# Attention followed by two MLPs on one core: scores of the 384- and 512-key tiles by head from fp32r parts, and products of zeros at the front

## The chip, the cores and the metric

One core of one Trainium2 chip. The metric is the device time of one execution in microseconds (us), as the median of three runs. TensorE is the matrix engine (PE in the rows, its weight loads PEld); DVE is VectorE, ACT is ScalarE, POOL is GpSimd, SP is the engine that issues most of the DMAs.

## The reference, cut to what matters

Three parts follow one another. Batch 4, 8 heads, 576 positions, 64 values per head; 2304 tokens of 512 values; hidden size 2048.

```python
scores = q @ k.T / sqrt(64)                    # per batch and head
scores = where(pos_i // 64 >= pos_j // 64, scores, -1e9)
attn   = softmax(scores);  x = attn @ v        # x: 2304 x 512 over the heads
h = x @ w_in;  g = s * relu(h)**2 + b;   x = g @ w_out      # first MLP
h = x @ w2_in; g = max(0.01*h, h);       out = g @ w2_out   # second MLP
```

The mask works on blocks of 64 positions: a query sees all keys of its own block and of the blocks before it.

## The kernel before, in words

**Tiles.** The 576 positions are cut into five tiles of 128 query positions, k = 0 to 4 (the last has 64). One tile over the four batches is a block of T = 512 tokens (256 for k = 4) of the MLPs. ORDER (line 165) runs ten blocks: the first MLP over the tiles 0, 1, 2, 4, 3, then the second over 0, 1, 2, 3, 4. Attention of a tile runs beside the first MLP of the block before it: attention of k = 1 beside block k = 0, k = 2 beside k = 1, k = 4 beside k = 2, and k = 3 (512 keys) beside block k = 4, the short one with T = 256. Only the attention of k = 0 has no MLP beside it; it is the front of the kernel (lines 467 to 545).

**MLP.** For each of 16 slices f of the hidden size, `m_in` (line 706) makes h with 12 products in fp32r (parts of x and of the weights, high and low: `xh`, `xl`; three products for each of four chunks), ScalarE and VectorE make from it the parts `gh` and `gl`, and `m_out` (line 751) makes 12 products into four banks y0 to y3 (line 765). The weights come as 64-bit words and are turned into parts by VectorE and ScalarE (`chunk`, lines 256 to 293). Results of the four y banks go through SBUF tiles `yo` of the pool "st" (line 777) to DRAM.

**Attention of a later tile** (`later_block`, line 552) is 16 units, one for each batch and pair of heads. The scores of a unit are fp32 products (`scores`, line 426; the profile shows two passes for each product). Two heads lie in one 128-row contraction: the tile `qz` holds for 64 query positions (half s of the tile) the columns of head 0 in its upper 64 rows and of head 1 in its lower 64 rows, with zeros elsewhere, so the 128 output rows are two heads times 64 positions. There is one product for each half, and it takes only the keys that this half sees: 320 and 384 for k = 2, 448 and 512 for k = 3. Each half has a PSUM bank of the pool "s" (two banks). Then come the maximum (line 391), its negative (394), exp with a running sum (400), 1/sum (406, 409), the product with it (422), transposes through bank "t" (445), their copy into `pt` (358, 360) and, for two units at once, the product with v (line 650), where the two heads write different halves of the output's partitions.

**Order.** A planner (class `Graph`, line 44) simulates the engines with costs written beside each step and takes, whenever an engine is idle, the ready step with the lowest due time; buffers are counted as in the pools. The sequence it finds is written out, and on the chip each engine runs its steps strictly in it. The cost estimates of attention (`att_pe`) and of the MLP blocks set the due times (`begin`).

**Front.** TensorE starts with 8 products of zeros (WARM, line 461) into the bank "h", which is also the bank of `m_in`; then come the four pairs of heads p of tile 0, whose scores stand in y0/y1, y2/y3, the two "s" banks, and y0/y1 again (line 511), with transposes through "t" and "h" and the product with v into "t".

Of the kernel before, what the change touches and what calls it, by code (L numbers as in the profile page):

```python
# [168 lines left out]
def kernel(  # L169
# [23 lines left out]
    scale = 1.0 / float(D) ** 0.5  # L193
    WARM, LATE, PACE, AHEAD = 8, 10, (6.0, 4.9), 3
    EARLY = NF - 1

    def sb(name, bufs):
        return ctx.enter_context(tc.tile_pool(name=name, bufs=bufs))

    def ps(name, bufs):  # L200
# [5 lines left out]
        "w": (sb("w", NF), NF), "st": (sb("st", 3), 3),  # L206
        "xf": (sb("xf", 4), 4), "xh": (sb("xh", 4), 4), "xl": (sb("xl", 4), 4),
        "g": (sb("g", 1), 1), "gh": (sb("gh", 2), 2), "gl": (sb("gl", 2), 2),
        "k": (sb("k", 2), 2), "v": (sb("v", 3), 3), "p": (sb("p", 2), 2), "pt": (sb("pt", 3), 3),
# [4 lines left out]
    G = Graph({k: n for k, (_, n) in pools.items()}, ("k", "v", "p", "pt", "s", "t", "h", "xf", "xh", "xl", "st"))  # L214
# [14 lines left out]
    qz = [const.tile([128, 2, 2, 64], F32, name=f"qz{i}") for i in range(3)]  # L229
# [4 lines left out]
    att_pe = [16 * (share[k] * 1.67e-3 + NQ[k] / 64 * (k + 1) * 0.21 + 0.15) for k in range(NB)]  # L234
# [118 lines left out]
    def memz(e, ap):  # L353
        e.memset(ap, 0.0)
# [9 lines left out]
    def both(n):  # L364
        return {"ACT": act(n), "DVE": dve(n)}

    qz_ok = [
        G.add({"POOL": 0.4}, lambda e, z=z: memz(e, z), due=14.0 if i else -99) for i, z in enumerate(qz)
    ]
    qz_free = [[q] for q in qz_ok]  # L370
# [90 lines left out]
    for i in range(WARM):  # L461
        G.add(
            {"PE": 0.43}, lambda e: e.matmul(out=wb()[:, :128], lhsT=qz[0][:, 0].rearrange("d h c -> d (h c)"),
                                             rhs=qz[0][:, 0].rearrange("d h c -> d (h c)"), start=True, stop=True),
            [qz_ok[0]], [wb] * (i == 0), [wb], -90,
        )
# [42 lines left out]
    for p in range(NP):  # L509
        due = 10.0 + 4.0 * p  # L510
        y0, y1 = [bank(key, "s") for key in (("y0", "y1"), ("y2", "y3"), ("s", "s"), ("y0", "y1"))[p]]
# [12 lines left out]
        tr = transposed(P, pcols, cells, pt, nrm, due, ("t", "h"))  # L524
        o = bank("t", "o")
# [24 lines left out]
    nq = [0]  # L550

    def later_block(blk):
# [5 lines left out]
        for u in range(NP * B):  # L558
            p, b = divmod(u, B)
            due = w0 + (u + 1) * (w1 - w0) / (NP * B)  # L560
            z = nq[0] % len(qz)
            nq[0] += 1
            K = buf("k", [128, S], F32)
            V = buf("v", [128, 5, 128], F32)
            ql = [
                G.add({"SP": 0.65}, lambda e, h=h, z=z, b=b, p=p: e.dma_start(
                    out=qz[z][64 * h:64 * h + 64, :ns, h], in_=qT[b, p, 64 * h:64 * h + 64, h, 128 * k:128 * k + NQ[k]].rearrange("d (s c) -> d s c", c=64)),
                    qz_free[z], due=due - 13, nbytes=32768)
# [20 lines left out]
            if k == 1:  # L589
                bk = bank("s", "s")  # L590
                cols = [(bk, 0, keys[0]), (bk, keys[0], keys[1])]
            elif k < NB - 1:
                cols = [(bank("s", "s"), 0, n) for n in keys]
            else:
                cols = None
            P = buf("p", [128, 1024], F32)
            q_ap = lambda j, z=z: qz[z][:, j].rearrange("d h c -> d (h c)")
            k_ap = lambda j, n, K=K: K()[:, :n]
            wide = nj * 128
            if cols:  # L600
                pads = G.add({"POOL": 0.2}, lambda e, P=P: memz(e, P()[:, keys[0]:keys[0] + 64]), [], [P], [], due - 6)
                sc = scores(k, [], [K], cols, q_ap, k_ap, [*ql, *kl], due, set())
                nrm = softmax(k, None, cols, P, [s * wide for s in range(ns)], due, sc)
                cells = [(s * wide + 128 * j, s) for j in range(nj) for s in range(ns)]
            else:
# [5 lines left out]
                for j in range(2):  # L611
                    def fn(e, j=j, bk=bk, K=K, z=z):
                        e.matmul(out=bk[j]()[:, :half], lhsT=qz[z][:, 0].rearrange("d h c -> d (h c)"), rhs=K()[:, half * j:half * j + half], start=True, stop=True)  # L613
                    sc.append(G.add({"PE": half * 1.67e-3 + 0.02}, fn, [*ql, *kl], [bk[j]], [K], due - 5))
# [20 lines left out]
            qz_free[z] = sc  # L635
# [9 lines left out]
            def av(e, pair=pair, o=o, n=n):  # L645
                for x, (b, V, pt, _) in enumerate(pair):
                    for j in range(nj):
                        for h in range(2):
                            r = pt()[:, j * ns * 128:(j + 1) * ns * 128].rearrange("k (s c) -> k s c", s=ns)[:, :, 64 * h:64 * h + 64]
# [208 lines left out]
```

## Time and profile before

| | us |
|---|---|
| median of three runs (lowest, highest) | 1018.62 (1015.87, 1020.55) |
| the profiled execution | 1019.93 |
| its span, from the first to the last instruction | 1018.1 |
| TensorE busy | 995.8 |
| VectorE, ScalarE, GpSimd busy | 452.9, 403.9, 93.3 |

The profile is of one execution. Its page gives the busy time of each engine and the same over 40 equal slices of the span, in tenths, with the clock granted to TensorE. The chain of waits follows the work that ended last back to its beginning, each piece with its start and its length; pieces of one line next to each other are merged. The timeline gives instructions in order of time. The length of a single matrix product in the timeline includes its way through the array, which overlaps the next one's; what a product costs in a dense row is the distance between starts, or the chain's piece divided by its count.

### The profile page before, as it was taken

The numbers are of one execution on the slowest core, as the hardware profiler recorded it, in microseconds if no ns is written. First come the engines' busy times: TensorE is split into PE (matmuls) and PEld (weight loads), VectorE is DVE, ScalarE is ACT, GpSimd is POOL, SyncE is SP. The second block draws the span as 40 slices with busy tenths as digits, with TensorE's granted clock in tenths as the row PEclk, the third lists the DMA queues.
The fourth block names the chain that finished last, engine by engine and source line by source line (L and its number), as shares of the span: only waits on it lengthen the run. The fifth ranks groups of instructions, "written<-read, shape, count | busy, mean of one in ns | idle before, by whom it ended". The sixth has DMA issues, their size and how long they took to land.

```text
span 1018.1 us, 14594 instructions
## 1 busy us (share of the span) xinstructions
PE 995.8 (98%) x5536; PEld 816.7 (80%) x5536; DVE 452.9 (44%) x855; ACT 403.9 (40%) x866; POOL 93.3 (9%) x238
## 2 busy tenths in 40 slices
PE   8799999999999999999999999999999999999997
PEld 7578787777777887777888888888888888888897
DVE  4889855443364434555455888413112211311211
ACT  3667754333353333443344766323122122222221
POOL 1021311111111111122310000000000000000000
PEclk7799999999999999999999999999999999999999
DMA  8872232222232333333324547002000200200010
GB/s 241 267 273 78 69 91 89 64 60 60 64 108 76 85 86 86 102 94 94 92 64 138 202 169 245 1 0 83 1 1 21 63 1 1 62 1 1 1 43 21
DMA packets 88645, 83.86 MB, mean 82 GB/s; under 512 B 28544, under 2 KB 71680, under 8 KB 88576
## 3 DMA queue, kind: packets, MB, share of 16 engines
q1 hardware_dynamic: 86128, 82.15, 26.1%
q10 hardware_dynamic: 2448, 0.79, 0.3%
q8 instruction: 44, 0.72, 0.3%
q14 instruction: 25, 0.20, 0.1%
HBM read 73.47 MB, written 9.44 MB: 81 GB/s over the span
## 4 chain that ended last, share of the span: by engine, by line
PE 92%; DVE 3%; ACT 2%; DMA 1%; issue 1%; POOL 0%; ACTq 0%; SPq 0%; DVEq 0%; POOLq 0%
PE h L716 38%; PE y L765 37%; PE s L430 6%; PE o L650 4%; PE t L445 4%; PE s L613 2%; PE o L530 1%; ACT p L400 1%; DVE nm L391 0%; DVE g L732 0%; POOL p L422 0%; DMA fk<-in_k_dram 0%; ACT g L734 0%; ACT w L279 0%; DMA fq<-in_q_dram 0%
## 5 line engine op out<-in xcount | busy, mean ns | idle before, releaser
L716 PE MATMUL h<-xh,w 128*128 128x512 f32 (+1 forms) x1280 | 455.6, 385 | 4.1 <-DVE g L732 2.0
L765 PE MATMUL y<-gh,w 128*128 128x512 f32 (+2 forms) x1280 | 369.4, 372 | 0.1
L716 PEld LDWEIGHTS h<-xh,w 128*128 128x128 f32 x1280 | 237.9, 189 | 55.2 <-DVE g L732 7.0
L765 PEld LDWEIGHTS y<-gh,w 128*128 128x128 f32 x1280 | 230.1, 188 | 41.8 <-issue 1.6
L765 PE MATMUL y<-gl,w 128*128 128x512 f32 (+2 forms) x640 | 236.2, 369 | 0.2 <-DVE gl L745 0.2
L716 PE MATMUL h<-xl,w 128*128 128x512 f32 (+1 forms) x640 | 235.9, 369 | 0.0
L745 DVE TENSOR_TENSOR gl<-g,gh 128x512 fp32r<-128x512 f32 (+1 forms) x80 | 51.0, 638 | 271.5 <-ACT g L744 271.5
L743 ACT ACTIVATE gh<-h 128x512 fp32r<-128x512 f32 (+1 forms) x80 | 44.3, 554 | 268.1 <-PE h L716 267.8
L716 PEld LDWEIGHTS h<-xl,w 128*128 128x128 f32 x640 | 121.0, 189 | 21.3 <-issue 2.6
L765 PEld LDWEIGHTS y<-gl,w 128*128 128x128 f32 x640 | 120.6, 188 | 21.1 <-DVE gl L745 0.4
L734 ACT ACTIVATE g<-h 128x512 f32<-128x512 f32 (+1 forms) x80 | 44.4, 555 | 135.7 <-PE h L716 134.7
L400 ACT ACTIVATE p<-s,nm 128x64 f32<-128x64 f32 (+7 forms) x128 | 62.8, 508 | 43.3 <-DVE nm L394 31.0
L422 POOL TENSOR_SCALAR p<-p,l 128x192 f32<-128x192 f32 (+3 forms) x95 | 59.0, 634 | 189.5 <-DVE l L409 136.0
L445 PE MATMUL t<-id_sb,p 128*128 128x128 f32 x400 | 67.1, 283 | 8.7 <-DVE p L415 5.5
L445 PEld LDWEIGHTS t<-id_sb,p 128*128 128x128 f32 x400 | 50.1, 145 | 29.5 <-issue 10.6
L430 PE MATMUL s<-k,qz 128*128 128x192 f32 (+2 forms) x192 | 70.8, 470 | 1.6 <-ACT p L400 1.5
L391 DVE TENSOR_REDUCE nm<-s 128x1 f32<-128x192 f32 (+3 forms) x104 | 53.4, 523 | 38.3 <-PE s L430 36.5
L732 DVE TENSOR_TENSOR g<-g,h 128x512 f32<-128x512 f32 (+1 forms) x52 | 32.8, 630 | 64.2 <-ACT g L734 63.8
L358 ACT ACTIVATE pt<-t 128x512 f32<-128x512 f32 (+2 forms) x67 | 33.7, 502 | 64.6 <-PE t L445 63.9
L360 DVE COPY pt<-t 128x512 f32<-128x512 f32 (+2 forms) x53 | 34.0, 641 | 52.0 <-PE t L445 51.6
L737 DVE TENSOR_TENSOR gl<-g,gh 128x512 fp32r<-128x512 f32 (+1 forms) x80 | 51.0, 637 | 11.7 <-ACT gh L736 10.2
L736 ACT ACTIVATE gh<-g 128x512 fp32r<-128x512 f32 (+1 forms) x80 | 47.1, 588 | 16.1 <-DVE g L732 14.6
(68 smaller groups left out, 709.8 us busy)
## 6 DMA issues: line engine op xcount, KB each, us to landing
early<-in_moe_w_in_dram SPq DMA_DIRECT2D x30, 512.0 KB, 3.8
early<-in_moe_w_out_dram SPq DMA_DIRECT2D x30, 512.0 KB, 4.8
v<-in_v_dram SPq DMA_DIRECT2D x32, 256.0 KB, 3.1
k<-in_k_dram SPq DMA_DIRECT2D x32, 144.0 KB, 2.8
yT<-yo SPq DMA_DIRECT2D x16, 256.0 KB, 2.2
k<-in_k_dram SPq DMA_DIRECT2D x32, 128.0 KB, 2.8
xf<-yT SPq DMA_DIRECT2D x16, 256.0 KB, 2.8
out_dram<-yo SPq DMA_DIRECT2D x16, 256.0 KB, 2.6
```

Of the source, the lines that this page charges most:

```text
L391: e.reduce_max(out=nm()[:, j:j + r], in_=i, axis=AX.X)
L400: e.activation(out=P()[:, pcols[j]:pcols[j] + n], in_=bk()[:, c:c + n], func=ACTF.Exp, bias=nm()[:, j:j + 1], scale=scale, accum_out=l()[: ...
L422: e.tensor_scalar(out=pp, in0=pp, scalar1=l()[:, j:j + 1], scalar2=1.0, op0=ALU.mult, op1=ALU.mult)
L430: e.matmul(out=bk()[:, c:c + n], lhsT=q_ap(j), rhs=k_ap(j, n), start=True, stop=True)
L445: e.transpose(tb()[:, x * 128:(x + 1) * 128], P()[:, pc:pc + 128], id_sb)
L716: e.matmul(out=h()[:, :T], lhsT=w()[:, wi, c * 128:(c + 1) * 128], rhs=x[blk, c]()[:, :T], start=(c == 0 and n == 0), stop=(c == KD - 1 an ...
L734: a = G.add({"ACT": act(T)}, lambda e: e.activation(out=g()[:, :T], in_=h()[:, :T], func=ACTF.Relu), [prev], [g], [h], due)
L736: hi = G.add({"ACT": act(T)}, lambda e: e.activation(out=gh()[:, :T], in_=g()[:, :T], func=ACTF.Copy), [a], [gh], [g], due)
L737: lo = G.add({"DVE": dve(T)}, lambda e: e.tensor_tensor(out=gl()[:, :T], in0=g()[:, :T], in1=gh()[:, :T].bitcast(F32), op=ALU.subtract), [ ...
L743: hi = G.add({"ACT": act(T)}, lambda e: e.activation(out=gh()[:, :T], in_=h()[:, :T], func=ACTF.Lrelu), [prev], [gh], [h], due)
L745: lo = G.add({"DVE": dve(T)}, lambda e: e.tensor_tensor(out=gl()[:, :T], in0=g()[:, :T], in1=gh()[:, :T].bitcast(F32), op=ALU.subtract), [ ...
L765: e.matmul(out=y()[:, :W], lhsT=w()[:, wi, d * 128:(d + 1) * 128], rhs=x()[:, :W], start=(f == 0 and n == 0), stop=(f == NF - 1 and n == 2),)
```

## The change

1. **Scores of k = 2 and k = 3 by head.** A unit loads q as it is (pool "q", 3 buffers; upper 64 rows head 0, lower 64 rows head 1) and k as before. ScalarE copies both into fp32r parts (`qs[:, 0]`, `kh`), VectorE subtracts for the low parts (`qs[:, 1]`, `kl`). Six products follow: for each of three pairs of parts one product of the upper 64 rows (head 0) and one of the lower 64 rows (head 1), each over all `nk` keys and with 128 query positions as output rows, the heads in a bank of "s" each. The 64 x 64 corner that the mask hides in each bank is overwritten with -1e30 by VectorE. Maximum, exp and the product with 1/sum run over `nk` keys for both heads. The pads of `p` fall away, and the product with v reads 128 columns in a row. `kh`, `kl` and `qs` have one buffer each.
2. **q of k = 1 and k = 4** keeps the layout with zeros, but in the rotating pool "q" too: GpSimd clears the tile before each load. The three constant tiles `qz` are gone.
3. **Products of zeros at the front.** After the 8 products of 128 columns, 26 more (FILL) of 256 columns, fp32, on a tile of zeros `wq` in the pool "g", with due time 60. All 34 hold the bank "h". The banks of the front are dealt anew: scores in y0/y1, y2/y3, y0/y1, y2/y3, transposes through "t" and "s", the product with v into "s".
4. **"st" has 2 buffers, not 3**, and the estimate `att_pe` for k = 2 and 3 is lower.

```diff
+    FILL = 26
-        "w": (sb("w", NF), NF), "st": (sb("st", 3), 3),
+        "w": (sb("w", NF), NF), "st": (sb("st", 2), 2),
...
+    wq = buf("g", [128, 512], F32, "wq")
+    wq_ok = G.add({"POOL": 0.4}, lambda e: memz(e, wq()), opens=[wq], due=-99)
-    for i in range(WARM):
+    for i in range(WARM + FILL):
+        n = 128 if i < WARM else 256
         G.add(
+            {"PE": n * 1.67e-3 * (2 if i < WARM else 1)}, lambda e, n=n: e.matmul(out=wb()[:, :n], lhsT=wq()[:, :128], rhs=wq()[:, :n], start=True, stop=True),
+            [wq_ok], [wb] * (i == 0), [wb, wq], -90 if i < WARM else 60,
...
-        y0, y1 = [bank(key, "s") for key in (("y0", "y1"), ("y2", "y3"), ("s", "s"), ("y0", "y1"))[p]]
+        y0, y1 = [bank(key, "s") for key in (("y0", "y1"), ("y2", "y3"), ("y0", "y1"), ("y2", "y3"))[p]]
-        tr = transposed(P, pcols, cells, pt, nrm, due, ("t", "h"))
-        o = bank("t", "o")
+        tr = transposed(P, pcols, cells, pt, nrm, due, ("t", "s"))
+        o = bank("s", "o")
...
+            flat = 2 <= k < NB - 1
+            Q = buf("q", [128, 256], F32, "q")
+            z = [] if flat else [G.add({"POOL": 0.45}, lambda e, Q=Q: memz(e, Q()), opens=[Q], due=due - 14)]
...
+                ok = [G.add({"ACT": act(128)}, lambda e, Q=Q, qs=qs: e.activation(out=qs()[:, 0], in_=Q()[:, :128], func=ACTF.Copy), ql, [qs], [Q], due=due - 7)]
+                ok.append(G.add({"DVE": dve(128)}, ... out=qs()[:, 1], in0=Q()[:, :128], in1=qs()[:, 0].bitcast(F32), op=ALU.subtract ...
+                ok.append(G.add({"ACT": act(nk)}, ... out=kh()[:, :nk], in_=K()[:, :nk], func=ACTF.Copy ...
+                ok.append(G.add({"DVE": dve(nk)}, ... out=kl()[:, :nk], in0=K()[:, :nk], in1=kh()[:, :nk].bitcast(F32), op=ALU.subtract ...
+                bk = [bank("s", "s") for _ in range(2)]
+                def fn(e, qs=qs, kh=kh, kl=kl_, bk=bk):
+                    o = [x() for x in bk]
+                    for n, (qc, kk) in enumerate(((0, kh), (0, kl), (1, kh))):
+                        for h in range(2):
+                            r = slice(64 * h, 64 * h + 64)
+                            e.matmul(out=o[h][:, :nk], lhsT=qs()[r, qc], rhs=kk()[r, :nk], start=(n == 0), stop=(n == 2))
+                for h in range(2):
+                    mk = G.add({"DVE": 0.22}, lambda e, x=bk[h]: e.memset(x()[:64, nk - 64:nk], NEG), [sc], uses=[bk[h]], due=due - 4.5)
+                    mx.append(G.add({"DVE": dve(nk)}, ... e.reduce_max(out=nm()[:, h:h + 1], in_=x()[:, :nk], axis=AX.X) ...
```

## Rows read from the trace of the kernel before

**Rows 1.** The page: busy time of engines, then granted clock in 40 slices.

```profile
PE 995.8 (98%) x5536; PEld 816.7 (80%) x5536; DVE 452.9 (44%) x855; ACT 403.9 (40%) x866; POOL 93.3 (9%) x238
...
PEclk7799999999999999999999999999999999999999
```

**Rows 2.** Busy time by stretch: length, PE, PEld, DVE, ACT, POOL, clock, DMA.

```profile
25.50:51.00 25.50, 19.46 (x107) 14.64 (x104) 22.31 (x43) 17.66 (x53) 1.69 (x4) 0.80 0.84 268
...
204.00:229.00 25.00, 25.00 (x152) 19.61 (x151) 10.34 (x27) 9.78 (x26) 4.62 (x12) 1.00 0.21 58
...
458.00:484.00 26.00, 24.81 (x191) 19.04 (x190) 14.45 (x35) 9.96 (x28) 7.16 (x20) 1.00 0.33 93
...
860.00:910.00 50.00, 50.00 (x222) 41.28 (x221) 12.44 (x18) 12.93 (x23) 0.00 (x0) 1.00 0.11 32
```

**Rows 3.** Chain of waits: start, length, piece; attention of k = 2, then k = 3.

```profile
181.57 1.46 PE o L650 x24
...
196.56 0.54 PE s L430 x2
...
197.31 0.65 PE s L430 x2
...
501.43 1.90 PE o L650 x32
503.33 0.55 PE h L716 x3
...
507.97 0.35 PE h L716 x3
508.32 0.75 PE s L430 x2
...
509.42 0.86 PE s L430 x2
```

**Rows 4.** Groups of instructions by line and shape: busy us, mean ns.

```profile
L737 DVE TENSOR_TENSOR gl<-g,gh 128x512 fp32r<-128x512 f32 x64 | 43.8, 685 | 10.0 <-ACT gh L736 9.2 <-PE y L765 0.7
L736 ACT ACTIVATE gh<-g 128x512 fp32r<-128x512 f32 x64 | 40.4, 631 | 13.2 <-DVE g L732 12.0
...
L391 DVE TENSOR_REDUCE nm<-s 128x1 f32<-128x512 f32 x16 | 11.1, 691 | 7.2 <-PE s L430 6.9
...
L354 POOL MEMSET qz<- 128x256 f32 x3 | 0.9, 313 | 0.3 <-POOLq L847 0.3
```

**Rows 5.** Timeline of ScalarE, one unit of k = 3: start, length, instruction.

```profile
511.57 0.64 ACT L400 ACTIVATE p<-s,nm 128x448 f32<-128x448 f32 x1 [0.22 <-DVE nm L394]
...
512.77 0.20 ACT L400 ACTIVATION_READ_ACCUMULATOR p<-s,nm 128x1 f32 x1
```

**Rows 6.** Timeline of TensorE at the front.

```profile
1.10 3.78 PE L463 MATMUL warm<-qz 128*128 128x128 f32 x16 [1.10 <-POOL qz L354]
5.75 5.86 PE L430 MATMUL s<-fk,fq 128*128 128x64 f32 x32 [0.87 <-DMA fq<-in_q_dram]
14.38 2.22 PE L445 MATMUL t<-id_sb,p 128*128 128x128 f32 x8 [2.77 <-DVE p L415]
...
16.85 1.98 PE L530 MATMUL o<-pt,fv 128*64 128x128 f32 x16
...
25.03 1.09 PE L530 MATMUL o<-pt,fv 128*64 128x128 f32 x16
```

**Rows 7.** Busy time of the front by stretches of 2 us, columns as in rows 2.

```profile
14.00:16.00 2.00, 1.57 (x7) 1.34 (x8) 0.94 (x3) 1.80 (x12) 0.00 (x0) 0.50 1.28 210
...
24.00:26.00 2.00, 2.00 (x26) 1.76 (x24) 1.81 (x5) 1.75 (x10) 0.19 (x1) 1.00 1.00 385
...
38.00:40.00 2.00, 2.00 (x17) 1.58 (x13) 1.83 (x2) 1.67 (x4) 0.00 (x0) 0.50 0.84 334
```

**Rows 8.** Timelines of VectorE: weights at the front, last copies at the tail.

```profile
45.17 1.23 DVE L282 TENSOR_TENSOR w<-early,w 128x1024 fp32r<-128x1024 f32 x1 [0.33 <-ACT w L279]
...
1014.60 0.42 DVE L360 COPY yo<-y 128x256 f32<-128x256 f32 x1 [1.70 <-DMA out_dram<-yo]
```

More of the change, by code (lines that the diff above doesn't have):

```diff
@@ L213 @@
     }
-    G = Graph({k: n for k, (_, n) in pools.items()}, ("k", "v", "p", "pt", "s", "t", "h", "xf", "xh", "xl", "st"))
+    G = Graph({k: n for k, (_, n) in pools.items()}, ("k", "kh", "kl", "q", "qs", "v", "p", "pt", "s", "t", "h", "xf", "xh", "xl", "st"))
     E = {"PE": nc.tensor, "DVE": nc.vector, "ACT": nc.scalar, "POOL": nc.gpsimd, "SP": nc.sync}
@@ L228 @@
     b_sb = const.tile([128, 1], F32, name="b_sb")
-    qz = [const.tile([128, 2, 2, 64], F32, name=f"qz{i}") for i in range(3)]
     yT = dr_p.tile([DM, NT], F32, name="yT")
     share = [sum(D * m for m in ([2 * k + 1, 2 * k + 2] if k < NB - 1 else [9])) for k in range(NB)]
-    att_pe = [16 * (share[k] * 1.67e-3 + NQ[k] / 64 * (k + 1) * 0.21 + 0.15) for k in range(NB)]
+    att_pe = [16 * ((3.5 * (128 * (k + 1) / 2400 + 0.013) + 0.24 if 2 <= k < NB - 1 else share[k] * 1.67e-3) + NQ[k] / 64 * (k + 1) * 0.21 + 0.15) for k in range(NB)]
     unit = [(3 * 2 * KD) * (n / 2400 + 0.013) for n in TB]
@@ L365, in both @@
         return {"ACT": act(n), "DVE": dve(n)}
[L367 to L370, printed above, removed]
+    NEG = -1e30
     ones_ok = G.add({"POOL": 0.1}, lambda e: e.memset(ones[:, 0:2], 1.0), due=14.0)
@@ L591, in later_block @@
                 cols = [(bk, 0, keys[0]), (bk, keys[0], keys[1])]
-            elif k < NB - 1:
-                cols = [(bank("s", "s"), 0, n) for n in keys]
             else:
@@ L601, in later_block @@
                 pads = G.add({"POOL": 0.2}, lambda e, P=P: memz(e, P()[:, keys[0]:keys[0] + 64]), [], [P], [], due - 6)
-                sc = scores(k, [], [K], cols, q_ap, k_ap, [*ql, *kl], due, set())
+                sc = scores(k, [Q], [K], cols, q_ap, k_ap, [*ql, *kl], due, set())
                 nrm = softmax(k, None, cols, P, [s * wide for s in range(ns)], due, sc)
@@ L611, in later_block, with fn @@
                 for j in range(2):
-                    def fn(e, j=j, bk=bk, K=K, z=z):
-                        e.matmul(out=bk[j]()[:, :half], lhsT=qz[z][:, 0].rearrange("d h c -> d (h c)"), rhs=K()[:, half * j:half * j + half], start=True, stop=True)
-                    sc.append(G.add({"PE": half * 1.67e-3 + 0.02}, fn, [*ql, *kl], [bk[j]], [K], due - 5))
+                    def fn(e, j=j, bk=bk, K=K, Q=Q):
+                        e.matmul(out=bk[j]()[:, :half], lhsT=Q()[:, :128], rhs=K()[:, half * j:half * j + half], start=True, stop=True)
+                    sc.append(G.add({"PE": half * 1.67e-3 + 0.02}, fn, [*ql, *kl], [bk[j]], [K, Q], due - 5))
                 nm, l = buf("sm", [128, 8], F32, "nm"), buf("sm", [128, 8], F32, "l")
@@ L643, in later_block, with av @@
             n = NQ[k]
-            def av(e, pair=pair, o=o, n=n):
+            def av(e, pair=pair, o=o, n=n, flat=flat):
                 for x, (b, V, pt, _) in enumerate(pair):
```

60 lines of the change are left out of this document (46 added, 14 removed).

## The prediction

> **What bounds the kernel now.** I read the page first. TensorE is busy for 995.8 of 1018.1 us, no other engine for half of the span, and the granted clock is below full in the first two slices only [rows 1]. The stretches say the same: beside the attention of k = 2 TensorE is busy in 25.00 of 25 us, beside that of k = 3 in 24.81 of 26, in the pure MLP in 50.00 of 50, but only in 19.46 of 25.5 between 25.5 and 51 us [rows 2]. So from about 50 us on a microsecond of TensorE's queue is a microsecond of the kernel, as long as the work around it keeps up; before that the chain runs through TensorE, ScalarE, VectorE and the loads in turn. The chain of waits then gives what a product costs in the queue [rows 3], since the timeline's lengths overlap.
>
> **The scores of k = 2 and 3, removed.** A unit of k = 3 has a piece of 0.75 us for the half with 448 keys and one of 0.86 us for 512; for k = 2 the pieces are 0.54 and 0.65 us [rows 3]. That is 1.61 and 1.19 us per unit, and over 16 units each 25.8 + 19.0 = 44.8 us of TensorE.
>
> **The scores, added.** Six fp32r products of `nk` columns. In the pure MLP 222 such products of 512 columns fill 50 us, 0.225 us each [rows 2], and three of 256 columns take 0.35 us, 0.117 each [rows 3]; 384 columns lie between, at 0.171. Whether the product of the upper 64 rows runs beside that of the lower 64 is the open question, since no operation of the trace uses half of the rows. The nearest row is the product with v, where the two heads use different halves of the columns: 24 and 32 passes take 1.46 and 1.90 us [rows 3], so one more pass of 128 columns costs 0.055 us. The same 128 columns in the scores cost 0.86 / 2 x 128 / 512 = 0.107 us, so the halves run side by side nearly fully (factor 1.95). The rows also show what entering and leaving that mode costs: 1.90 - 32 x 0.055 = 0.14 us within, and the three MLP products behind it take 0.55 us in place of 0.35, 0.34 us together. I charge each score step these 0.34 us.
>
> The bounds: pairs at full overlap with no change of mode cost 3 x 0.225 = 0.68 and 3 x 0.171 = 0.51 us, a gain of 16 x (0.93 + 0.68) = 26 us. One after the other, with the mode, they cost 1.69 and 1.37 us, a loss of 16 x (0.08 + 0.18) = 4 us. I take the overlap of the product with v, as it is the same mechanism with the other axis of the array split, its 0.34 us, and half a product more for the ends of the row of six, where one half works alone: 1.13 and 0.94 us, a gain of 0.48 and 0.25 us per unit, **11.7 us** in all.
>
> The Trainium skill speaks for less. Its page "TensorE: Matmul & The Clock Gate", section "Measured speedup vs the span model", gives 3.07 for four row tiles where 4 would be ideal. An estimate from that share of 0.77 would make a pair 0.29 us at 512 columns and the gain about 9 us; the trace here has only the 1.95 of the column halves, and none of the row halves.
>
> **What feeds the scores.** Each unit gets a ScalarE copy of 512 (384) columns and one of 128, and VectorE differences of the same size. The rows of the same forms are 0.63 and 0.69 us at 512 [rows 4]; with 128 columns I take 0.3 us each. Two memsets of 64 x 64 in PSUM have no row; VectorE's copy of 256 columns takes 0.42 us [rows 8], so 0 to 0.4 each, and I take 0.2. VectorE gets 1.4 us more per unit and ScalarE 0.9. They lie beside TensorE's MLP work: beside k = 2 VectorE and ScalarE are busy for 10.34 and 9.78 of 25 us [rows 2] and a unit comes every 8 us, so the cost there is nothing. If this cover were gone, a unit would wait for 1.3 us of copy and difference ahead of its scores.
>
> Beside k = 3 it is tight. VectorE is busy for 14.45 of 26 us [rows 2]; a unit comes every 6.3 us (16 between 408 and 509 us), so it takes 3.5 us of VectorE per unit, and 4.9 after, in a period that shrinks to about 5.8: 84% busy. The two "s" banks are now opened by one step and freed by its last exp. Their cycle is 1.1 (scores) + 2 x 0.2 (memset) + 2 x 0.69 (maxima [rows 4]) + 1.40 (both exps, 511.57 to 512.97 [rows 5]) and some 0.5 for the negative and the hand-overs, 4.8 us, and each MLP step of VectorE or ScalarE that gets between adds 0.4. Queued behind a late maximum on VectorE are the MLP's own `g` and `gl`, and TensorE waits for these. Before, one half could start while the other's bank was still being read; that is gone. I charge 2 us of new idle time for the 16 units; the bounds are 0 and 7.7, the whole gain of k = 3.
>
> **The front.** TensorE's clock is at 1.2 GHz, a granted 0.50, from 14 to 24 us and from 31 to 40 [rows 7]: it fell after idle stretches such as the 2.77 us ahead of 14.38 [rows 6]. The same 16 passes of the product with v take 1.98 us there and 1.09 at 25 us, at 2.4 GHz [rows 6]. Between 14.4 and 24 us TensorE has little idle time, so at the full clock this stretch would be some 4 to 4.5 us shorter. From 24 to 46 us VectorE is the slower one (22.31 of 25.5 us [rows 2]): it makes the weights of slice 1, ready at 46.4 [rows 8], so of the second low stretch nothing is gained, but the first moves VectorE's whole row forward.
>
> Against it stand the 26 products. One of 256 columns is twice 256 columns of the scores' price, 0.43 us at the full clock, 11 us together. The six idle times ahead of products between 5 and 40 us, two of them in [rows 6], add up to 8.2 us, and at the full clock there would be more, so most of them fit. The first do not: the planner sees idle time ahead of the first scores, puts about four there, and on the chip these begin at the low clock and end near 7.4 us, where the scores started at 5.75 before; these scores then run faster (5.86 us for 32 passes before [rows 6]), which leaves them 0.6 us late. I take **3.5 us** gained; the bounds are a gain of 6 and, if nothing lifts the clock, the loss below.
>
> The banks dealt anew cost nothing: p = 2 and 3 take y0 to y3, which the exps of p = 0 and 1 have left before p = 2 is at its turn on TensorE. The MLP cannot start before the last product of zeros, as all hold "h"; it cannot start before x is there either, and the planner has used them up by then.
>
> **q of k = 1 and 4.** GpSimd gets 32 memsets of 0.31 us [rows 4] and is busy for 9% of the span. The q loads wait for them on SP's queue, and with them the k and v loads and the weights behind; they are due 14 us ahead, so I take nothing. If POOL stood behind a late product with 1/sum, each would delay SP by about a microsecond.
>
> **"st" with 2 buffers.** At the tail the fourth copy waits 1.70 us for the first store [rows 8]. With two buffers the third waits so, and the fourth for the second store, one issue later: 0.6 us. At the nine block ends inside, the third copy comes about 2 us later, while `m_in` of the next block (2.7 us) covers it; 0.5 us in all, bounds 0 and 3.
>
> **The sum.** -11.7 (scores) + 2 (idle beside k = 3) - 3.5 (front) + 1.1 (stores) = -12.1. The profiled execution is 1019.93 us, its span 1018.1; that gives 1007.8. It stands 1.3 us above the median of 1018.62, from which the sum gives 1006.5. I forecast 1007.
>
> **Rivals.** (a) *Beside k = 3 VectorE and the banks set the pace.* The k = 3 gain is lost: 1019.9 - 12.1 + 7.7 - 2 = 1013.5. For it: 84% busy, and a bank cycle of 4.8 us and more in a period of 5.8. Against it: the planner sees these costs and reorders. (b) *The products of zeros don't lift the clock.* The 8 at the start ran for 3.78 us, and it stayed low until about 10 us, in the midst of the first scores, so the trace leaves it open. At the low clock 26 of them are 22 us against 8.2 idle: some 7 to 14 us lost at the front, 1019.9 - 8.6 + 10 = 1021. The Trainium skill ("TensorE: Matmul & The Clock Gate", section "What's actually happening") has the clock set by how busy the engine was, which speaks against this rival; the first 4.9 us of the trace neither show nor refute it. (c) *The halves run one after the other.* The place is the score step, the price 1.69 and 1.37 us per unit, and it decides as soon as a pair costs more than 1.8 single products: +4.2 + 2 - 3.5 + 1.1 = +3.8, 1022 to 1024, slower than before. For it: the halves write the same 128 partitions, in two banks, which no row shows. (d) *The change does more than I give it*: no price for the mode, about 1000.
>
> **How the numbers follow.** Forecast 0.60 (1002 to 1011), a 0.13, b 0.08, c 0.11, d 0.08. A measurement of this kernel can tell about 0.5%, 5 us, from no change. Faster by more: the forecast, d, half of a and a little of b, 0.76; slower by more: a third of b and of c, 0.07; between, 0.17. The range reaches from d to past a, and leaves out c and most of b: 999 to 1016.
>
> **What would show it.** The chain's pieces for a score step of k = 3: near 1.0 to 1.2 us for six products (c: 1.6); TensorE's idle time between 400 and 500 us: 2 to 5 us (a: 8 and more); the clock full from about 6 to 30 us and the weights of slice 1 ready near 43 us (b: half clock, and 50 or later). The prediction would be wrong if the planner's new order put stalls into stretches that are full now.

## The result and the profile after

The changed kernel takes 1000.53 us in the median of six runs (998.55 to 1001.27), the kernel before 1018.74 beside it (1015.87 to 1020.55). The ratio is 0.9825, with an interval of 0.9808 to 0.9842, so 16 to 20 us were gained; the forecast was 1007 us, a gain of about 12. The profiled execution took 1001.26 us, its span is 999.4 us.

The page of the changed kernel, busy time of TensorE and granted clock in 40 slices, to be held against [rows 1]:

```profile
PE 983.4 (98%) x5652; PEld 812.5 (81%) x5652; DVE 471.7 (47%) x973; ACT 433.8 (43%) x943; POOL 96.5 (10%) x233
...
PEclk9999999999999999999999999999999999999999
```

TensorE is busy for 12.4 us less, and no slice is at the low clock. The chain of waits, beside the attention of k = 2 and then of k = 3 (start, length, piece), answers to [rows 3]:

```profile
201.03 0.73 PE s L621 x6
201.76 0.89 PE h L766 x3
202.65 0.69 PE y L815 x3
...
449.43 0.89 PE s L621 x6
450.32 0.59 PE t L442 x4
...
456.73 0.44 PE t L442 x4
```

One piece of six products stands where two pieces of 0.54 and 0.65, or 0.75 and 0.86 us, stood. What comes behind it pays as well: three h products take 0.89 instead of 0.69 us, four transposes 0.59 instead of 0.44. With that, a step costs 0.73 + 0.20 = 0.93 us for k = 2, and 0.89 + 0.15 to 0.20, about 1.07 us, for k = 3; before it was 1.19 and 1.61, with nothing to pay behind it. By the pieces 16 units of each gain 16 x (0.26 + 0.54) = 12.8 us. TensorE's timeline of the same k = 3 step shows why:

```profile
449.36 0.50 PE L621 MATMUL s<-kh,qs 64*128 64x512 f32 x2
449.70 0.40 PE L621 MATMUL s<-kl,qs 64*128 64x512 f32 x2
449.93 0.39 PE L621 MATMUL s<-kh,qs 64*128 64x512 f32 x2
```

Each row is a pair, one product from the upper and one from the lower 64 rows. Its two starts lie 3 to 4 ns apart, and from the second pair to the third it is 0.23 us: a pair costs what one product of 512 columns costs in the pure MLP, 0.225 us.

The busy time of one stretch that holds the attention of k = 3 (length, TensorE, its weight loads, VectorE, ScalarE, GpSimd, clock), of the kernel before:

```profile
400.00:560.00 160.00, 155.73 (x1110) 125.50 (x1107) 82.98 (x185) 66.38 (x158) 29.72 (x82) 1.00 0.33 99
```

and of the changed one:

```profile
400.00:560.00 160.00, 155.77 (x1157) 131.12 (x1156) 102.67 (x245) 93.89 (x209) 26.43 (x61) 1.00 0.37 118
```

TensorE idles for 4.3 us in one and 4.2 in the other, though VectorE does 20 us and ScalarE 27 us more. Some 13 and 9 us of that are the rounding of weights for later slices, more of which falls into the same stretch now; the rest is attention. Between 400 and 500 us alone TensorE idles for 3.3 us before and 2.9 after. The planner has also given ScalarE ten of VectorE's copies into `pt`; the groups of 400 to 560 us, before and after:

```profile
L360 DVE COPY pt<-t 128x512 f32<-128x512 f32 x19 | 13.1, 691 | 12.0 <-PE t L445 11.7
...
L360 DVE COPY pt<-t 128x512 f32<-128x512 f32 x9 | 6.2, 692 | 7.6 <-PE t L442 7.6
```

The groups by line of what feeds the scores, over the whole run:

```profile
L607 ACT ACTIVATE qs<-q 128x128 fp32r<-128x128 f32 x32 | 9.8, 307 | 26.5 <-PE s L621 17.4 <-issue 8.3 <-ACT gh L786 0.4
L608 DVE TENSOR_TENSOR qs<-q,qs 128x128 fp32r<-128x128 f32 x32 | 9.0, 280 | 0.0
L627 DVE MEMSET s<- 64x64 f32 x64 | 6.2, 112 | 15.1 <-PE s L621 14.5
```

The front, TensorE's timeline against [rows 6] (`warm` are the products of zeros; a product of 256 columns is two passes):

```profile
8.09 1.95 PE L427 MATMUL s<-fk,fq 128*128 128x64 f32 x16
...
23.64 4.91 PE L464 MATMUL warm<-wq 128*128 128x256 f32 x22
28.39 1.04 PE L442 MATMUL t<-id_sb,p 128*128 128x128 f32 x8
...
31.88 0.48 PE L766 MATMUL h<-xh,w 128*128 128x512 f32 x1
```

and its weights of slice 1 on VectorE's timeline, against the 45.17 of [rows 8]:

```profile
39.53 1.22 DVE L282 TENSOR_TENSOR w<-early,w 128x1024 fp32r<-128x1024 f32 x1
```

The first h product starts at 31.88 us instead of 40.0; the step that completes the weights begins 5.6 us earlier, and they are ready at 40.75. TensorE runs nothing but products of zeros until 8.09 us, and the clock rises to 2.4 GHz among them: the starts of two passes of 256 columns lie 0.43 us apart until 6.6 us and 0.22 us from 7.0 on. Between 40 and 46 us the granted clock is 0.72 on average; it fell after TensorE waited 1.70 us for these weights ahead of 39.35 and 0.72 us ahead of 40.81.

**Where the time went.** The first copy of y into `yo` marks the end of a block. ScalarE's timeline of the changed kernel has three of the marks:

```profile
285.12 0.69 ACT L358 ACTIVATE yo<-y,s_sb 128x512 f32<-128x512 f32 x1 [0.53 <-PE y L815]
...
409.15 0.69 ACT L358 ACTIVATE yo<-y,s_sb 128x512 f32<-128x512 f32 x1 [0.52 <-PE y L815]
...
508.29 0.47 ACT L358 ACTIVATE yo<-y,s_sb 128x256 f32<-128x256 f32 x1
```

The table takes the same rows of each kernel's trace (us). The second column is the time to the first mark; the next ones are the distances to the second mark (beside it runs the attention of k = 2), to the third (k = 4), and over the two that follow. These last belong together: part of the work passes from one side of the mark between them to the other. Behind these the distances of all kernels agree within 0.5 us, but for the last block of `e1_no_fill`, `e2_front_only` and `e6_no_heads`, which is 0.7 to 1.0 us longer. Within the 0.5 us one difference is regular: the block behind these columns takes 86.4 us in every kernel with two `yo` buffers and 86.1 with three.

| kernel | front and block 0 | with k = 2 | with k = 4 | with k = 3, and the next |
|---|---|---|---|---|
| before | 161.67 | 132.51 | 124.71 | 199.95 |
| changed | 158.31 | 126.81 | 124.03 | 189.93 |
| `e2_front_only` | 163.60 | 130.69 | 124.66 | 199.98 |
| `e4_st_two` | 160.31 | 132.38 | 124.63 | 199.05 |
| `e5_same_half` | 159.17 | 134.55 | 124.72 | 199.65 |
| `e6_no_heads` | 158.92 | 131.40 | 124.61 | 198.83 |
| `e7_only_k3` | 157.84 | 131.44 | 124.81 | 189.93 |
| `e9_front_28` | 157.26 | 131.33 | 124.61 | 199.97 |

The second column moves by up to 3.4 us between executions of one front (158.31, 159.17 in `e5_same_half`, and 155.75 in `e3_heads_apart`, whose first block is planned alike). A part of that stands already at the first h product (31.88, 30.90 and 30.79 us). Another goes with the granted clock: all three wait 1.7 and 0.7 us for the weights of slice 1 near 39 us, and behind these waits the clock stays full in `e3_heads_apart`, falls to 0.50 for a part of the stretch in the changed kernel, and for all of it in `e5_same_half`:

```profile
40.00:46.00 6.00, 6.00 (x31) 4.88 (x31) 5.50 (x12) 4.87 (x10) 2.80 (x5) 1.00 1.00 301
...
40.00:46.00 6.00, 5.28 (x19) 4.19 (x19) 5.54 (x12) 3.91 (x10) 2.04 (x5) 0.72 0.99 320
...
40.00:46.00 6.00, 6.00 (x17) 4.77 (x18) 4.56 (x10) 3.32 (x7) 2.06 (x5) 0.50 1.03 313
```

The other columns are steady to some tenths.

### The profile page after: what moved, and what is told of

It is laid out like the page before. It is cut to its first block, busy times and chain, and to the rows that moved or that the text cites. A ratio compares the mean times of both kernels' runs of the same rounds, so it can differ in the third digit from the quotient of the medians.

```text
span 999.4 us, 15180 instructions
## 1 busy us (share of the span) xinstructions
PE 983.4 (98%) x5652; PEld 812.5 (81%) x5652; DVE 471.7 (47%) x973; ACT 433.8 (43%) x943; POOL 96.5 (10%) x233
## 4 chain that ended last, share of the span: by engine, by line
PE 96%; DVE 2%; ACT 1%; issue 0%; POOL 0%; DMA 0%; SPq 0%; POOLq 0%; ACTq 0%; DVEq 0%
PE h L766 40%; PE y L815 39%; PE t L442 5%; PE o L700 5%; PE s L621 2%; PE s L427 2%; PE warm L464 2%; PE s L661 2%; ACT g L784 0%; PE o L530 0%; DVE g L782 0%; DVE w L282 0%; ACT pt L358 0%; DVE early L266 0%; DMA out_dram<-yo 0%
## 5 line engine op out<-in xcount | busy, mean ns | idle before, releaser
L766 PE MATMUL h<-xh,w 128*128 128x512 f32 (+1 forms) x1280 | 448.2, 380 | 6.0 <-DVE g L782 2.2
L442 PEld LDWEIGHTS t<-id_sb,p 128*128 128x128 f32 x400 | 47.5, 141 | 18.7 <-ACT pt L358 3.8
L782 DVE TENSOR_TENSOR g<-g,h 128x512 f32<-128x512 f32 (+1 forms) x48 | 29.8, 620 | 57.5 <-ACT g L784 57.5
L642 POOL TENSOR_SCALAR p<-p,l 128x384 f32<-128x384 f32 (+1 forms) x60 | 38.2, 648 | 171.5 <-DVE l L640 149.8
L358 ACT ACTIVATE pt<-t 128x512 f32<-128x512 f32 (+2 forms) x69 | 36.0, 521 | 35.7 <-PE t L442 34.9
L700 PEld LDWEIGHTS o<-pt,v 128*64 128x64 f32 x896 | 40.9, 137 | 10.3 <-ACT pt L358 3.5
L360 DVE COPY pt<-t 128x512 f32<-128x512 f32 (+2 forms) x51 | 31.0, 608 | 38.2 <-PE t L442 37.9
L700 PE MATMUL o<-pt,v 128*64 128x128 f32 (+1 forms) x896 | 47.8, 258 | 0.1
L633 ACT ACTIVATE p<-s,nm 128x384 f32<-128x384 f32 (+1 forms) x64 | 39.9, 631 | 10.7 <-DVE nm L630 10.7
```

The costliest lines, as they stand in the source:

```text
L358: e.activation(out=out, in_=in_, func=ACTF.Copy, scale=by)
L442: e.transpose(tb()[:, x * 128:(x + 1) * 128], P()[:, pc:pc + 128], id_sb)
L633: G.add({"ACT": act(nk, 1, True)}, lambda e, h=h, nm=nm, l=l, P=P, bk=bk: e.activation(out=P()[:, nk * h:nk * h + nk], in_=bk[h]()[:, :nk] ...
L642: G.add({"POOL": pool(nk), "DVE": dve(nk, 2)}, lambda e, h=h, l=l, P=P: e.tensor_scalar(out=P()[:, nk * h:nk * h + nk], in0=P()[:, nk * h: ...
L700: e.matmul(out=o()[64 * h:64 * h + 64, n * x:n * x + n], lhsT=V()[:, j, 64 * h:64 * h + 64], rhs=r, start=(j == 0), stop=(j == nj - 1),)
L766: e.matmul(out=h()[:, :T], lhsT=w()[:, wi, c * 128:(c + 1) * 128], rhs=x[blk, c]()[:, :T], start=(c == 0 and n == 0), stop=(c == KD - 1 an ...
```

## The experiments

The theory: the scores gain because the two halves of the rows work at the same time, and the front gains because the products of zeros keep the clock up. The rivals: the gain comes from elsewhere than the halves; the front's lead is lost in the first MLP block; the order that the planner makes, not the clock, decides there.

**The scores: do the halves have to alternate?** `e3_heads_apart`:

```diff
-                    for n, (qc, kk) in enumerate(((0, kh), (0, kl), (1, kh))):
-                        for h in range(2):
+                    for h in range(2):
+                        for n, (qc, kk) in enumerate(((0, kh), (0, kl), (1, kh))):
```

> The changed kernel with the six products of a score step in another order: all three of head 0, then all three of head 1, so that two products next to each other mostly use the same 64 rows. Theory, the halves run side by side: a step loses two thirds of its overlap, 0.45 us for k = 3 and 0.34 for k = 2, 12 to 13 us for 32 units, 1012 to 1014 us, and the chain's piece of a step grows from 0.89 to about 1.35 us (0.72 to 1.06). Rival, the gain comes from fp32r and not from the halves: the pieces and the time stay, 1000 to 1001 us.

Measured: 999.51 us, ratio 0.9812 (0.9791 to 0.9833). Nothing was lost. TensorE's timeline of a k = 3 step:

```profile
435.19 0.51 PE L621 MATMUL s<-kh,qs 64*128 64x512 f32 x2
435.52 0.40 PE L621 MATMUL s<-kl,qs 64*128 64x512 f32 x2
435.75 0.40 PE L621 MATMUL s<-kh,qs 64*128 64x512 f32 x2
```

In the program the row is kh, kl, kh of head 0 and then kh, kl, kh of head 1. In the trace it is three pairs again, kh, kl, kh, the starts of a pair 10 ns apart. The trace names the operand of a product and not its head, but this sequence leaves one reading: the first product of head 1 starts ahead of the second and third of head 0. So my expectation fell, and with it the test: an order in the program can't make the halves run one after the other. This needed another edit.

**The scores: take the halves away.** `e5_same_half` has both heads read the upper 64 rows:

```diff
-                            r = slice(64 * h, 64 * h + 64)
+                            r = slice(0, 64)
```

> The changed kernel with both heads' six products of a score step fed from the upper 64 rows (both heads read head 0's rows, so the scores of head 1 are replaced by head 0's: that part of the computation is changed). Everything else stands as it was: the same count of products, the same banks, the same work beside. Theory (the gain of the scores is that the two heads' products run at the same time in the two halves of the rows): six products now follow one another, 6 x 0.225 = 1.35 us at 512 columns and 6 x 0.171 = 1.03 us at 384, in place of three pairs, 0.69 and 0.51 us; 16 steps of each give 16 x (0.66 + 0.52) = 19 us, so 1000.5 + 19 = 1019 us, with a range of 1012 to 1021 since the six may cost less than the column products did. In the trace the chain's score piece at k = 3 goes from 0.89 to about 1.5 us and the second product starts some 0.2 us behind the first, not a few ns. Rival (the gain is only in fp32r parts and fewer products, not in halves running together): within 2 us of the changed kernel, 999 to 1003 us.

Measured: 1020.27 us, ratio 1.0014 (1.0002 to 1.0026). The chain, a step of k = 2 and one of k = 3:

```profile
204.57 1.25 PE s L621 x6
...
433.59 1.57 PE s L621 x6
```

The pieces grew by 0.52 and 0.68 us, 19.2 us over 16 units of each, and the time by 19.7. All that the scores gain is the halves' running together; six fp32r products of half of the rows, one after the other, are worth no more than the fp32 products were (by the table the k = 2 column is 3.1 us longer than with the old scores of `e6_no_heads`, that of k = 3 0.8).

**The scores: size by size.** `e6_no_heads` is the changed kernel with the old scores, `e7_only_k3` has the new ones for k = 3 alone:

```diff
-            flat = 2 <= k < NB - 1
+            flat = False        # e6_no_heads
+            flat = k == 3       # e7_only_k3
...
+            elif k < NB - 1 and not flat:
+                cols = [(bank("s", "s"), 0, n) for n in keys]
```

(the estimate `att_pe` follows `flat`).

> The changed kernel with the scores of the 384 and 512 key tiles as before (whole fp32 products of all rows against zero-padded q), but with the front, the rotating q tiles that GpSimd clears, and two st buffers of the change. Theory (the scores are worth about 14 us, the front about 5 of the 18 only where the first MLP block runs behind it without waits, which the rotating q tiles and the order give): 1000.5 + 14 = 1014 us, and the fronts of the first MLP block's later products (start of the second block near 155 us) as in the changed kernel. Rival (it is the by-head scores that let the front's lead stay, through the order that the planner makes with them): 1018 to 1021 us, as with the front alone, and the second block starts near 160 us again.

> The changed kernel with by-head scores for the 512 key tiles alone, those of 384 as before. Theory (each step's gain is the difference of the score pieces: at k = 3 about 0.53 us by 16 and at k = 2 about 0.35 us by 16, 8.5 and 5.5 us): 1000.5 + 5.5 = 1006 us, 1004.5 to 1007.5. By the document's own terms (k = 3 7.7 us, k = 2 4.0) it would be 1004.5. Rival (the gain is not in the steps but in what VectorE and the banks free beside them, k = 3 above all): within 1.5 us of the changed kernel.

Measured: 1015.93 us, ratio 0.9970 (0.9957 to 0.9983), and 1004.94 us, ratio 0.9867 (0.9842 to 0.9891), the first 2 us above its theory, the second within its range. So the rest of the change is worth 1.7 to 4.4 us, k = 2 about 4.4 and k = 3 about 11. The table sharpens this: from `e6_no_heads` to the changed kernel the column of k = 2 falls by 4.6 us, and the next one by 0.6, as in every kernel whose k = 2 scores run in pairs; to `e7_only_k3` the last column falls by 8.9; 1.0 us more of the difference is the last block of `e6_no_heads`. The chain of `e7_only_k3` has an old k = 2 step, with nothing to pay behind it:

```profile
201.82 1.19 PE s L427 x4
203.01 0.22 PE t L442 x2
```

**The store tiles.** `e4_st_two` is the kernel before with `"st": (sb("st", 2), 2)`.

> The kernel before with two yo buffers in place of three and nothing else. Theory: 0.6 us at the tail and next to nothing inside, 1019 to 1020 us. Rival, the later copies hold VectorE or TensorE at the nine block ends: 0.3 us and more each, 1021.5 us and above.

Measured: 1018.17 us, ratio 0.9993 (0.9978 to 1.0008): no difference. The trace shows three that cancel: the last column is 0.9 us shorter with the order that was planned for two buffers, the block behind it 0.3 us longer, and behind the first copy of the last block the span ends 7.06 us later instead of 6.37. VectorE's last copies in the changed kernel show the same end:

```profile
992.35 0.42 DVE L360 COPY yo<-y 128x256 f32<-128x256 f32 x1 [0.48 <-PE y L815]
995.19 0.42 DVE L360 COPY yo<-y 128x256 f32<-128x256 f32 x1 [2.41 <-DMA out_dram<-yo]
995.87 0.42 DVE L360 COPY yo<-y 128x256 f32<-128x256 f32 x1 [0.25 <-DMA out_dram<-yo]
```

**The front: without the products of zeros, and alone.** `e1_no_fill` is the changed kernel with `FILL = 0`; `e2_front_only` is the kernel before with the third part of the change alone.

> The changed kernel without its 26 products of zeros (FILL = 0; the 8 of before stay, and the banks of the front stay dealt anew). Theory, the clock: the 26 products keep TensorE at 2.4 GHz through the front, so without them the granted clock falls to 0.50 in the wait for the first exps again, the scores of p = 0 run at the low clock, and the weights of slice 1 are ready 3 to 5 us later than the 40.8 us of the changed kernel; 1004 to 1006 us. Rival, the banks: the front is shorter because transposes and the product with v go through other banks; then the time stays within 1 us of the changed kernel's 1000.5. Rival, the products of zeros stand in the way: 998 to 1000.

> The kernel before with the front of the change alone: 26 products of zeros and the banks dealt anew; scores, q loads and the yo buffers as before. Theory: 3 to 5 us gained at slice 1 and most of it kept, 1014 to 1016 us. Rival: VectorE sets the pace of the first MLP block, the gain of the front is given back there, and the time is within 1 us of 1018.7.

Measured: 1005.66 us, ratio 0.9873 (0.9853 to 0.9893), and 1020.62 us, ratio 1.0016 (1.0002 to 1.0029), the first as the clock theory had it, the second not the 1014 to 1016 expected. Without the products the changed kernel loses 5 us, and the whole front is worth nothing in the kernel before. In `e1_no_fill` the clock is low as expected: the 16 passes of the product with v at 17.31 us take 1.98 us, those of the changed kernel at 17.34 take 1.09, and the step that completes the weights of slice 1 begins at 43.40 instead of 39.53. But its order is planned anew too. In `e2_front_only` the clock is full from 7 to 40 us, and the first h product starts at 30.3 us. And still nothing is left of it. What TensorE waits for there between 28 and 76 us, the two longest (total, times, longest):

```profile
PE t L446 <- POOL p L423: 2.8, 2, 2.1
PE y L769 <- ACT gh L740: 2.0, 1, 2.0
```

None of these waits is in the changed kernel. GpSimd's timeline has the reason of the first: two normalising products of a unit, which take 1.17 us at this point of the changed kernel, take 4.24,

```profile
62.73 4.24 POOL L423 TENSOR_SCALAR p<-p,l 128x192 f32<-128x192 f32 x2 [2.03 <-DVE l L410]
```

The order of the first block is another, too: products of y stand ahead of products of h, and wait for `gh`. Two things were open: is it this order that takes the lead, and is it the clock or the order that gives the 5 us? What the banks dealt anew are worth alone was not run.

**The front: two products fewer.** `e8_fill24` is the changed kernel with `FILL = 24`.

> The changed kernel with 24 products of zeros at the front in place of 26. In the trace of the changed kernel the last stretch of them ends at 28.39 us, while the weights of the third pair that its transposes wait for are ready near 27.45 us: the products of zeros hold the transposes by nearly 1 us. Theory (the front's end is on the path): two less, 2 x 0.22 us, let the MLP begin 0.4 us earlier, 1000.1 us, and the clock stays full. Rival (VectorE's rounding of the weight slices paces the MLP's first steps): no change, 1000.5 us within 0.5. Both are near what this measurement can tell, so the trace is what tells: the start of the first h product, 31.88 us, and the end of the waits for slice 1.

Measured: 1006.68 us, ratio 0.9881 (0.9859 to 0.9903): 6 us lost for two products of zeros, which neither theory expected. (One such product is two passes, so two of them are 0.88 us, not the 0.44 that I wrote.) The front itself went as expected: the transposes start at 27.69 instead of 28.39, the first h product at 30.48, and the clock is full:

```profile
14.00:24.00 10.00, 10.00 (x92) 9.16 (x91) 7.61 (x18) 6.28 (x30) 0.30 (x2) 1.00 1.02 285
24.00:32.00 8.00, 7.27 (x49) 6.00 (x48) 7.09 (x18) 6.57 (x29) 0.00 (x0) 1.00 1.01 311
```

The two longest waits of TensorE between 28 and 76 us are those of `e2_front_only`:

```profile
PE t L442 <- POOL p L419: 2.4, 2, 1.6
PE y L815 <- ACT gh L786: 2.0, 1, 2.0
```

From 16 to 25 products of zeros the planner of the changed kernel makes one and the same order, with 26 to 28 another. The count works through the plan.

**The same order, other lengths; another order, the same front.** In the next four kernels one of the two is held. `e9_front_28` is `e2_front_only` with `FILL = 28`, from which the planner makes the other order. In `e10_short_fills`, `e12_half_fills` and `e11_tiny_fills` the 26 products of the changed kernel run over 192, 128 and 16 columns, but are planned as 256, so each engine's order is the changed kernel's:

```diff
-            {"PE": n * 1.67e-3 * (2 if i < WARM else 1)}, lambda e, n=n: e.matmul(
+            {"PE": n * 1.67e-3 * (2 if i < WARM else 1)}, lambda e, n=min(n, 192): e.matmul(
```

> The kernel before with the front of the change, as e2_front_only, but with 28 products of zeros in place of 26. With that count the planner lays the first MLP block out as in the changed kernel (products of h first, then y), where with 26 it put products of y first, which waited 2.03 us for gh at 40 us, and gave GpSimd a normalise that held the transposes 2.8 us near 65 us. Theory (the front is worth some 3 to 4 us in this kernel too, and what took it away was the planned order of the first block, not the kernel around): 1015.5 us, 1014 to 1017, with the second block's products 4 us ahead of the kernel before. Rival (the rotating q tiles are what keeps the lead): 1019 to 1021 us, as with 26.

> The changed kernel with its 26 products of zeros cut to 192 columns each in place of 256, planned as if they still had 256, so the order of every engine is the changed kernel's. Their time falls by a quarter, from 0.44 to 0.33 us each, more than the two that were left out in e8_fill24 (24 x 0.44 = 10.6 us, here 26 x 0.33 = 8.6 us). Theory (e8's 6 us came from the order that the planner made with 24, not from less work at the front): 999.5 to 1001.5 us, perhaps 0.5 us below the changed kernel since the transposes of the third pair start up to 0.9 us earlier. Rival (the clock or the start needs the whole length of the 26 products): 1004 to 1007 us, as with 24.

> The changed kernel with its 26 products of zeros cut to 16 columns each, planned as if they still had 256, so the order of every engine stays the changed kernel's while TensorE is idle where they stood. The run without any products of zeros, 1005.66 us, had another planned order too, so it left open whether the clock or the order was worth its 5 us. Clock theory (the order is not enough: without the products TensorE waits at the front, the clock falls as in the kernel before, and the weights of slice 1 come late): the granted clock near 0.5 for parts of 14 to 36 us, and 1002.5 to 1006 us. Order theory (the planned order alone gave the gain, as the run with 24 full products suggests, whose clock was full and which still lost 6 us): 999 to 1001.5 us.

> The same with the 26 products at 128 columns, half their length, planned as with 256. By the clock theory this lies between the short ones and the tiny ones: some idle time at the front, the clock mostly full until 30 us, 999 to 1002 us; if the transposes' start is on the path, up to 1 us below the changed kernel. By the order theory: the same 999 to 1001.5 us; the two differ in the granted clock of 24 to 36 us more than in the time.

Measured:

| kernel | median, us | ratio to before | first h product, us | first mark, us |
|---|---|---|---|---|
| `e9_front_28` | 1015.15 | 0.9968 (0.9954 to 0.9981) | 31.57 | 157.26 |
| `e10_short_fills` | 999.24 | 0.9807 (0.9781 to 0.9833) | 29.91 | 156.36 |
| `e12_half_fills` | 998.01 | 0.9801 (0.9784 to 0.9818) | 31.42 | 156.36 |
| `e11_tiny_fills` | 1005.38 | 0.9873 (0.9855 to 0.9890) | 34.12 | 160.66 |

The busy time of TensorE and the clock, `e11_tiny_fills`:

```profile
14.00:24.00 10.00, 8.76 (x66) 7.93 (x64) 4.59 (x11) 2.47 (x7) 0.30 (x2) 0.66 0.98 249
24.00:32.00 8.00, 6.88 (x54) 6.28 (x54) 6.54 (x18) 7.92 (x37) 0.00 (x0) 0.85 1.05 343
```

and `e12_half_fills`:

```profile
14.00:24.00 10.00, 9.75 (x97) 9.09 (x98) 8.06 (x20) 6.68 (x30) 0.30 (x2) 1.00 1.03 276
24.00:32.00 8.00, 6.24 (x44) 5.26 (x43) 6.09 (x14) 5.32 (x22) 0.00 (x0) 0.79 0.81 262
```

`e9_front_28` and `e10_short_fills` came near the times of the order theory (1015.5, and 999.5 to 1001.5), `e11_tiny_fills` within the range of the clock theory (1002.5 to 1006), and `e12_half_fills` 1 us below the range of both. So both causes are real. With the order held, taking the products' length away costs 4.9 us by the medians (2.1 between the two profiled executions): the granted clock falls to 0.66 between 14 and 24 us, where VectorE and ScalarE then get 3.0 and 3.8 us less done than with the changed kernel's products (7.63 and 6.28 us there), and the first h product comes 2.2 us later. With a full clock at the front in all four, from 7 to 40 us, the other order costs as much or more: `e8_fill24` against `e10_short_fills`, 7.4 us, and `e2_front_only` against `e9_front_28`, 5.5 us. A part of that is the clock again, later on: at the waits for GpSimd's product the clock falls once more in both kernels with the other order (to 0.50 for 3.4 us, from 68.8 us in `e8_fill24` and from 68.0 in `e2_front_only`) and stays full in the changed one. The same stretch in `e8_fill24` and in the changed kernel:

```profile
66.00:74.00 8.00, 5.61 (x31) 3.92 (x30) 3.34 (x5) 1.62 (x2) 3.36 (x3) 0.79 0.36 143
...
66.00:74.00 8.00, 8.00 (x47) 6.35 (x46) 7.19 (x9) 5.70 (x7) 0.15 (x1) 1.00 0.71 240
```

The rotating q tiles play no part, since `e9_front_28` has the old ones. And half of the length is enough: `e12_half_fills` is the fastest kernel of all, 2.5 us below the changed one by the medians, with intervals that still overlap a little.

## Why the prediction was right, point by point

The forecast of 1007 us with its range of 999 to 1016 held the sign, and the range held the time. The mechanisms of the scores and of the clock stood as told: the chain's piece for k = 3 (0.89 us, about 1.07 with what follows it), TensorE's idle time between 400 and 500 us (2.9 us) and the full clock (from 7 us to beyond 30) came where I had said they would, the weights of slice 1 somewhat before (40.75 us, not near 43). The sum was 6.6 us too small, though: 12.1 us from the profiled execution, where the two spans differ by 18.7. The median of 1000.5 us lies just outside the 1002 to 1011 that I gave 0.60, where I had placed rival (d). By terms, in the columns of the table:

- **Scores, 11.7 forecast, 14.1 measured** (4.6 for k = 2 in its own column and 0.6 in the next, 8.9 for k = 3). The price of the mode was nearly right: 0.34 us forecast; 0.35 to 0.42 is seen, 0.20 to 0.22 within a step and 0.15 to 0.20 behind it. The pairs at full overlap were right too. What failed is the half product for the ends of the row: the starts of a pair lie 3 ns apart, no half ever works alone, and the 0.11 and 0.09 us by 16 that I charged, 3.2 us, aren't there; the price of the mode being a little higher gives 2 us of that back. That makes the 12.8 us of the chain's pieces; the columns have 1.3 us more, which the pieces don't explain. Rival (c) stood on the halves running one after the other. `e5_same_half` makes that case, and its 1020.27 us are near the 1022 to 1024 worked out for it. An estimate from the 3.07 of 4 in the Trainium skill ("TensorE: Matmul & The Clock Gate", section "Measured speedup vs the span model") would have made a pair 0.29 us and the gain about 9 us; here two halves gave 2 x 0.225 / 0.23 = 1.95 of 2, so the trace does not agree with that estimate, and the measurement decides.
- **Idle time beside k = 3, 2 us lost forecast, none measured** (4.2 us against 4.3). VectorE was charged too much. A memset takes 0.112 us, not 0.2; the planner moved ten copies into `pt` to ScalarE, which the sum had left with VectorE; and the score steps of k = 3 come every 6.2 us (6.7 before), not every 5.8 (6.3). Between 433 and 458 us VectorE is busy for 16.68 of 25 us, 67%, not the 84% worked out. Rival (a) falls with it.
- **Stores, 1.1 us lost forecast, 0.1 gained** in the profiled executions, and no difference by the medians of `e4_st_two`. The tail's 0.6 us are there (0.7), and of the 0.5 inside 0.3; but the last column is 1.1 us shorter than the scores make it (0.9 in `e4_st_two`), by the order that was planned.
- **Front, 3.5 us forecast, 4.5 measured** in the spans (3.4 in the first column and 1.1 in the second, which is as much shorter in `e6_no_heads` and `e9_front_28`, without the new scores), or 3.8 us by the medians of `e9_front_28` and the kernel before beside it. The size is right within what one execution can show. That products of zeros lift the clock is shown by the distances of their starts (0.43 us, then 0.22), that they hold it by `e11_tiny_fills`, and rival (b) falls. The Trainium skill (the same page, section "What's actually happening") has the clock follow how busy the engine was; the kernels with one order agree with that: where TensorE had idle time in place of the products, the granted clock was 0.66 between 14 and 24 us instead of 1.00.

The misses add up: 2.4 + 2.0 + 1.2 + 1.0 = 6.6 us. Three of the four hold prices that I put in for caution, all on one side. Rival (d), about 1000 us without any price for the mode, gives the time that came, but not for its reason: the price is there, and other prices are not.

What I had not seen, though I named it last as what would make the prediction wrong, is how much hangs on the order. The 3.5 us of the front were argued from the clock alone, and that they came is in part luck. The run of the front alone shows that a front with the full clock and the first h product 10 us earlier can be worth nothing; the changed kernel has 6 of its 18 us because 26 lies in the narrow span of counts from which the planner makes the good order. The planner's own simulated end has the sign of this, if not the size: 994.0 us with 26 products in the changed kernel and 995.2 with 24; 1004.6 in the kernel before, 1006.0 in `e2_front_only` and 1004.1 in `e9_front_28`. What exactly tips it between 25 and 26 stays open.

## What to carry to other kernels

Here two products of 64 rows each into banks of their own cost as much as one (0.23 us at 512 columns), and each step of such products amid whole ones costs 0.35 to 0.42 us on top; price it so, and don't add for ends. Three pairs at a time paid: a step went from 1.61 to 1.07 us with 512 keys, from 1.19 to 0.93 with 384. Where a planner writes out the order, a change at the front has two effects, its own and that of the new order, and a run in which one is held (here: products planned at one length and run at another) tells them apart. Where the planner simulates a time, that is a first sign. A front that begins 10 us earlier proves nothing until the end of the first block is read.

## What the runs showed of the hardware that was not expected

- **Products in different halves of the rows don't wait for their turn in the program.** In `e3_heads_apart` the first product of the second head starts 10 ns behind that of the first head, ahead of two products that precede it in the program. Interleaving them by hand changed nothing that the medians can tell (1000.53 us with it, 999.51 without). The Trainium skill ("TensorE: Matmul & The Clock Gate", section "The mechanism") says that products start strictly in the order of the program; for different halves of the rows this trace shows otherwise.
- **Products of zeros lift and hold the clock**: in the changed kernel it rises at 7.0 us with nothing else run before, and is 1.00 from 8 to 40 us. In `e12_half_fills`, with half the columns, it is still 1.00 from 14 to 24 us and 0.79 from 24 to 32, and the kernel loses nothing by it.
- **GpSimd's product with 1/sum varies widely**: a pair of 128 x 192 took 1.17 us in the changed kernel (at 63.34 us, where VectorE has a gap of 0.73) and 4.24 and 4.87 us in the two kernels with the other order (at 62.73 and 64.34 us, beside VectorE's rounding of weights without a gap). That VectorE holds it was not tried.
- **The front varies by up to 3.4 us from one execution to another of one order, while the distances behind it repeat within some tenths.** The granted clock behind the same two waits near 39 us was 1.00, 0.72 and 0.50 between 40 and 46 us in three executions, and the first mark came at 155.75, 158.31 and 159.17. Small effects are better read from the distances between marks than from spans.
